# Two pairs of local attention and gated MLP on one core: Q and K of three blocks computed up front, and the head sums of block 0 made on VectorE

## The chip, the cores and the metric

The kernel runs on one core of one Trainium2 chip. The metric is the device time of one execution in microseconds. Before the change it is 1622.94 us, the median of 9 runs (1622.45 to 1624.91).

## The reference

There are two layers with residuals, A and B, and the pair runs twice over the same x of shape [1, 2048, 1024] in bf16:

```python
qkv = (x @ wqkv).reshape(B, S, 3, H, Dh)       # H = 32 heads of Dh = 32
idx = pos[:, None] - arange(8)[None, :] * 2    # W = 8 keys at distance 0, 2, ... 14
logits = einsum("bhsd,bhswd->bhsw", q, k[idx]) * Dh ** -0.5
attn = softmax(where(idx >= 0, logits, -1e9))
A(x) = einsum("bhsw,bhswd->bhsd", attn, v[idx]) @ wo
B(x) = ((x @ W_gate) * (x @ W_gate > 0) * (x @ W_up)) @ W_down     # F = 3584
x = x + A(layernorm(x));  x = x + B(layernorm(x))      # and both once more
```

A position sees only 8 keys behind it, so the scores are no matrix product: for each head, position and key 32 products are made and summed.

## The kernel before

**Tiling.** The 2048 tokens are cut into 4 blocks of 512 (NB = 4, four tiles of 128 tokens each). A block of one pair is a number n: 0 to 3 are the first pair, 4 to 7 the second (NN = 8). A PE group is eight matmuls of 128x128 by 128x512, which together give one 128x512 accumulator out of six in PSUM. x stays in SBUF. Weights come in slabs of 1 MB through a ring of five buffers (`wring`, `slab_events` L213).

**Attention of a block.** `ln_steps` (L225) normalizes the tiles, on ScalarE or for some on VectorE (`ln_dve_stats` L279, its reciprocal root on GpSimd at L294), and a DMA transposes the result to `xnT`. `qk_steps` (L464) makes 8 chunks of Q and 8 of K, one PE group each, with ScalarE copying q (L479) and k (L483) out of PSUM, and GpSimd copying the 14 columns of halo that a K chunk takes from the block before and leaves for the next (L485 to L488). `v_steps` makes V, which goes through DRAM (`v_d`) to a head-major layout (`load_v_steps` L617).

The scores are sums over 32 rows out of the eight chunks. Each row of a chunk holds one of 4 slices of a head, so the sum over chunks can be made elementwise, and the last sum over 4 rows on PE with the 0/1 matrix `sel`, or by two sums on VectorE after a trip through DRAM. There are three variants:

- block 0: `prod_direct_steps` (L509) makes one bf16 product of 128x4096 for each chunk on VectorE, and PE sums all eight with `sel` (`red_mm` L494, two times four chunks of eight matmuls);
- block 1: `prod_sum_steps` (L530) makes float32 products of half that size and adds them up on VectorE in two halves (L546, L548, L558). The last addition writes the bf16 tile `s`, and PE sums this with one `red_mm`;
- later blocks: the same sums, then `s` goes to DRAM and comes back in another layout (`store_s` L562, `load_s` L567, called s4 there), and VectorE adds the four slices (`head_sum` L578).

Then `softmax_steps` (L585), `pv_steps` (L631: products with V and their sums on VectorE), and the way through DRAM (`o_d`, `store_o` L659, `load_o` L668) to `oT`, which the output projection `wo_steps` (L679) needs.

**MLP of a block.** `gu_steps` (L702) runs 28 pairs of a gate group and an up group. ScalarE makes r = relu(gate), VectorE multiplies with up into `hT` (L103 on the page). `down_steps` (L727) sums over the 28 chunks of `hT` in two halves of D and adds the result to x (L758).

**The order of the work.** Each step is a Python function with a planned time. `emit` (L778) sorts all steps by it and calls them. Each engine therefore gets its instructions in this order, and some queues are held to it strictly: PE (`pe_group`, `mm`, L122 to L130), SyncE, which issues nearly all DMAs (`sp_dma` L113 to L119), and those VectorE instructions that go through `dv` (L98 to L103). The others are placed by a scheduler. The plan counts 1.73 us for a PE group (`GRP` L782). The order of the PE stages is: V0, QK0, QK1, V1, V2, output projection 0, V3, gate/up 0, QK2, output projection 1, down 0, gate/up 1, QK3, output projection 2, down 1, gate/up 2, QK4, V4, output projection 3, down 2, and so on. The schedule is at L788 to L913.

Of the kernel before, what the change touches and what calls it, by code (L numbers as in the profile page):

```python
# [13 lines left out]
P = 128  # L14
# [22 lines left out]
def kernel(  # L37
# [46 lines left out]
    pool = {}  # L84
    early_guard = tc.tile_pool(name="early", bufs=3)
    pool["early"] = early_guard.__enter__()

    def start_hidden():
        early_guard.__exit__(None, None, None)
        del pool["early"]  # L90
        pool["hid"] = ctx.enter_context(tc.tile_pool(name="hid", bufs=1))
# [19 lines left out]
    gate = [None]  # L111
# [45 lines left out]
    o_d = dram.tile([NT, H, DH, P], BF16, name="o_d")  # L157
    s_d = [dram.tile([P, W * BLK], BF16, name=f"s_d{i}") for i in range(2)]
# [31 lines left out]
    def want_qk(key, end):  # L190
        for i, nm in enumerate(("q", "k")):
            for hh in range(2):
                want((key, nm, hh), wqkv_v[:, hh * (KC // 2):(hh + 1) * (KC // 2), i * D:(i + 1) * D], end)
# [12 lines left out]
    def want_down(n, at, gap):  # L206
        for half in range(2):
            for s in range(NSL):
                rows = slice(8 * s, min(8 * (s + 1), FC))
                end = at + gap * (half * FC + min(8 * (s + 1), FC))  # L210
                want(("d", n, half, s), wd_v[:, rows, half * SLAB:(half + 1) * SLAB], end)
# [13 lines left out]
    def ln_steps(n, which, early=False, dve=()):  # L225
# [3 lines left out]
        def stats(t):  # L229
            def f():  # L230
# [6 lines left out]
                if t in dve:  # L237
                    hold[t] = ln_dve_stats(xt, which == "a")
                    return
# [11 lines left out]
        def apply(t):  # L251
            def f():
                if t in dve:
                    mv, rstd = hold[t]
                    if which == "a":
                        dv(nc.vector.tensor_scalar, hold["xn"][:, t, :], x_tiles[b * TPB + t][:], mv[:, 0:1], rstd[:],
                           op0=ALU.subtract, op1=ALU.mult)
                        return
                    gate[0] = nc.vector.tensor_scalar(hold["xn"][:, t, :], x_tiles[b * TPB + t][:], mv[:, 0:1], rstd[:],
                                                      op0=ALU.subtract, op1=ALU.mult).ins  # L260
                    return
# [17 lines left out]
    def ln_dve_stats(xt, ordered):  # L279
        def run(f, *args, **kwargs):  # L280
            if ordered:
                dv(f, *args, **kwargs)
            else:
                f(*args, **kwargs)

        bst = stat_pool.tile([P, 2, 6], F32, tag="bst", name="bst")
        run(nc.vector.bn_stats, bst[:, 0, :], xt[:, 0:512])
        run(nc.vector.bn_stats, bst[:, 1, :], xt[:, 512:1024])
        mv = stat_pool.tile([P, 2], F32, tag="mv", name="mv", bufs=4)
        run(nc.vector.bn_aggr, mv[:], bst[:].rearrange("p a b -> p (a b)"))  # L290
        vpe = stat_pool.tile([P, 1], F32, tag="vpe1", name="vpe1")
        run(nc.vector.tensor_scalar, vpe[:], mv[:, 1:2], EPS, None, op0=ALU.add)
# [171 lines left out]
    def qk_steps(n, ln, key):  # L464
        b = n % NB
        st = att[n]

        def f_(nm, c):
            def f():
                if nm == "q" and c == 0:  # L470
                    khalo[n] = qk_pool.tile([P, KC, HALO], BF16, tag="kh", name=f"kh_{n}", bufs=2)
# [5 lines left out]
                if nm == "q":  # L477
                    q = qk_pool.tile([P, BLK], BF16, tag="q", name=f"q_{n}_{c}")
                    tail_act[0] = nc.scalar.copy(q[:], acc[:]).ins  # L479
                    st[("q", c)] = q  # L480
                else:
                    k = qk_pool.tile([P, HALO + BLK], BF16, tag="k", name=f"k_{n}_{c}")
# [6 lines left out]
                    st[("k", c)] = k  # L489
            return f  # L490

        return [f_(nm, c) for nm, c in (QK_FIRST if n == 0 else QK_ORDER)]

    def red_mm(n, prod, first, last):  # L494
        st = att[n]
        if first:
            st["L"] = psum_l.tile([P, W, P], F32, tag="L", name=f"L_{n}")
        with pe_group():
            for wh in range(2):
                for tq in range(TPB):  # L500
                    mm(st["L"][32 * tq:32 * tq + 32, WH * wh:WH * (wh + 1), :], lhsT=sel[:],
                       rhs=prod[:, WH * wh:WH * (wh + 1), tq * P:(tq + 1) * P],
                       start=first, stop=last, skip_group_check=True, tile_position=(0, 32 * tq))
# [4 lines left out]

    def prod_direct_steps(n):  # L509
        prods = {}  # L510

        def mult(c):
            def f():
                if c in (3, 4):
                    prods[c] = work.tile([P, W, BLK], BF16, tag="t", name=f"prod_{c}")
                else:
                    prods[c] = big_tile([P, W, BLK], f"prod_{c}")
                i0, i1 = qk_bcast(n, c, 0, W)
                dv(nc.vector.tensor_tensor, prods[c][:], i0, i1, op=ALU.mult)
            return f  # L520

        def red(c0, c1):
            def f():
                for c in range(c0, c1):
                    red_mm(n, prods.pop(c), c == 0, c == KC - 1)
            return f

        return [mult(c) for c in range(KC)], [red(0, KC // 2), red(KC // 2, KC)]

    def prod_sum_steps(n):  # L530
        st = att[n]

        def mult(h, c):
            def f():
# [9 lines left out]
                if n == 1:  # L544
                    with tc.issue_after(gate[0]):
                        nc.vector.tensor_tensor(t[:], i0, i1, op=ALU.mult)  # L546
# [8 lines left out]
        def add(h, c):  # L555
            ac, t = st["ac"], st.pop(("t", c))
            o = st["s"][:, WH * h:WH * (h + 1), :] if c == KC - 1 else ac[:]
            nc.vector.tensor_tensor(o, ac[:], t[:], op=ALU.add)  # L558
# [72 lines left out]
    def pv_steps(n):  # L631
# [14 lines left out]
        def adds(g0):  # L646
            def f():
# [6 lines left out]
                gate[0] = tail_dve[0]  # L654
# [24 lines left out]
    def wo_steps(n):  # L679
# [3 lines left out]
        if n > 0:  # L683
            order = [(t, half) for half in range(2) for t in range(TPB)]

        def f_(i):
            def f():
                for t, half in order[2 * i:2 * i + 2]:
                    xt = x_tiles[b * TPB + t]
                    acc = psum.tile([P, BLK], F32, tag="acc", name="acc_wo")  # L690
                    with pe_group():
                        for c in range(KC):
                            mm(acc[:], lhsT=st["oT"][:, c, t, :], rhs=slab[("o", n, half)][:, c, :],
                               start=(c == 0), stop=(c == KC - 1))
                    xs = xt[:, half * SLAB:(half + 1) * SLAB]
                    nc.vector.tensor_tensor(xs, acc[:], xs, op=ALU.add)  # L696
            return f

        return [f_(t) for t in range(TPB)]


    def gu_steps(n, ln):  # L702
        hold = {}

        def f_(j):
            def f():
# [3 lines left out]
                accs = {}  # L710
                for nm in ("g", "u"):
# [5 lines left out]
                    accs[nm] = acc  # L717
                    if nm == "g":
                        r = pool["hid"].tile([P, BLK], BF16, tag="r", name="r", bufs=3)
                        with tc.issue_after(tail_exp[0]):  # L720
                            tail_act[0] = nc.scalar.activation(r[:], acc[:], ACT.Relu).ins  # L721
                dv(nc.vector.tensor_tensor, hold["hT"][:, j, :], accs["u"][:], r[:], op=ALU.mult)
            return f

        return [f_(j) for j in range(FC)], hold

    def down_steps(n, hold):  # L727
# [3 lines left out]
        def f_(half, s8):  # L731
            cols = [(t, 0, SLAB) for t in range(TPB)]
            if n == NN - 1 and half == 1:
                cols[-1:] = [(TPB - 1, 0, SLAB // 2), (TPB - 1, SLAB // 2, SLAB)]

            def f():
# [8 lines left out]
                ac = accs[half]  # L745
                nfc = min(8, FC - 8 * s8)
                wsl = slab[("d", n, half, s8)]
                for a, (t, c0, c1) in zip(ac, cols):
# [5 lines left out]
                if s8 == NSL - 1:  # L754
                    for a, (t, c0, c1) in zip(ac, cols):
                        xt = x_tiles[b * TPB + t]
                        xs = xt[:, half * SLAB + c0:half * SLAB + c1]
                        nc.vector.tensor_tensor(xs, a[:, c0:c1], xs, op=ALU.add)  # L758
                        if n == NN - 1:
                            row = (b * TPB + t) * P  # L760
                            col = half * SLAB + c0
                            dst = out_dram[row:row + P, col:col + c1 - c0]
                            if half == 1 and t % 2 == 1 and c0 == 0:
                                nc.scalar.dma_start(dst, xs)
                            else:
                                sp_dma(dst, xs)
            return f

        return [f_(half, s8) for half in range(2) for s8 in range(NSL)]
# [12 lines left out]
    GRP = 1.73  # L782

# [19 lines left out]
    def ln2(n, ats, turn_at=None, dve=()):  # L803
        stats, apply, turn, hold = ln_steps(n, "b", False, dve)
        ln_b[n] = hold
        for t, a in enumerate(ats):
            ev.append((a, stats[t]))
            ev.append((a + (4.0 if n == 0 else 12.0), apply[t]))
            if turn_at is None:
                ev.append((ats[-1] + 1.0 + 1.3 * t, turn(t)))  # L810
        if turn_at is not None:
            ev.append((turn_at, turn()))


    GAP0 = 1.9
    t_v0 = 9.5
    t_qk0 = t_v0 + GRP * KC
    t_qk1 = t_qk0 + GAP0 * 2 * KC
    t_v1 = t_qk1 + GRP * 2 * KC + 1.5
    t_v2 = t_v1 + GRP * KC  # L820
    t_wo0 = t_v2 + GRP * KC
    t_v3 = t_wo0 + GRP * KC
    t_gu0 = t_v3 + GRP * KC

    want_v("v0", t_v0 + GRP * 5, t_qk0)
    want_qk("qk01", t_v1)
    want_v("v123", t_v3 + GRP * KC / 2, t_gu0)
    for at, f in v_first(ln_a[0]):
        ev.append((t_v0 + at, f))
    ev.append((t_v0 + GRP * 5 + 0.5, lambda: load_x(1)))  # L830
# [3 lines left out]
    for t in range(TPB):  # L834
        ev.append((t_qk0 + (1.0, 2.0, 2.2 * GAP0, 4.2 * GAP0)[t], stats[t]))
        ev.append((t_qk0 + (1.9 + 2 * t) * GAP0 - 0.1, apply[t]))
        ev.append((t_qk0 + (1.9 + 2 * t) * GAP0, turn(t)))
    ev.append((t_qk0 + 1.5, store_v(0)))
    ev.append((t_qk0 + 18.0, lambda: load_x(3)))
    spread(qk_steps(0, ln_a[0], "qk01"), t_qk0, GAP0)  # L840
    mults, reds = prod_direct_steps(0)
    for c in range(KC):
        ev.append((t_qk0 + GAP0 * (2 * c + 2.0), mults[c]))
# [103 lines left out]
```

## Time and profile before

| | |
|---|---|
| median of 9 runs | 1622.94 us |
| the profiled execution | 1623.03 us |
| its span, first to last instruction | 1621.3 us |
| granted TensorE clock | 1.00 of full |
| DMA moved | 309.39 MB, 191 GB/s |
| `prod` of block 0 on VectorE | 8 x 2290 ns |
| `pv` products with V | 64 x 2286 ns |
| `x` plus output projection | 64 x 684 ns |
| gate product `hT` | 224 x 688 ns |

The profile is one execution with every instruction's start and length. A page gives each engine's busy time and share of the span, the chain of work that ended last (followed back from the last instruction, at each step to what released it), and groups of instructions by line, engine and tile. A group reads: line, engine, operation, output <- inputs, partitions x elements and type, count | busy us, mean ns | idle us of the engine just before them and what ended most of it. A timeline line reads: start us, length us, engine, line, operation, tiles, shape, count, and in brackets the idle time before it. Where a helper such as `mm` (L130) or `dv` (L103) records everything, all have its line, and the tile's name tells them apart. PE lengths overlap, since matmuls are pipelined: starts are to be compared with starts.

### The profile page before, as it was taken

To read this page: it belongs to the slowest core of one execution; us is meant where nothing else is said; L and a number is where in the kernel's file an instruction comes from. 1 tells how busy PE (TensorE), PEld (TensorE's weight loads), DVE (VectorE), ACT (ScalarE), POOL (GpSimd) and SP (SyncE) were. 2 spreads that over 40 slices of the span, in tenths; PEclk is the share of its full clock that TensorE was granted. 3 is DMA by queue.
4 is the path that set the end of the run, shared out by engine and by line. 5 is a ranking of instruction groups with operands and counts; after the bars stand their busy time and mean duration, and the time that the engine had idled before them with its cause. 6 is when DMAs were issued, how large, how long until landed. Compare 5 with 4: busy or idle time off the path is not lost.

```text
span 1621.3 us, 18791 instructions
## 1 busy us (share of the span) xinstructions
PE 1614.9 (100%) x7618; PEld 785.5 (48%) x7618; DVE 1085.4 (67%) x939; ACT 506.2 (31%) x1051; POOL 250.7 (15%) x220
## 2 busy tenths in 40 slices
PE   9999999999999999999999999999999999999999
PEld 6644445444544445444454444544445444444444
DVE  5799799959496857929579294892949929411211
ACT  4764323513252313613136031360313301131110
POOL 2321006400351002200053000530005100000000
PEclk9999999999999999999999999999999999999999
DMA  9589556776479585684757947579574894655452
GB/s 301 111 210 241 163 175 201 192 208 207 130 216 227 156 234 180 181 225 157 224 179 188 241 152 225 159 204 248 171 227 155 199 252 157 208 165 173 156 166 68
DMA packets 398006, 309.39 MB, mean 191 GB/s; under 512 B 167648, under 2 KB 377952, under 8 KB 396256
## 3 DMA queue, kind: packets, MB, share of 16 engines
q1 hardware_dynamic: 397344, 307.62, 66.9%
q8 instruction: 59, 0.97, 0.3%
q10 hardware_dynamic: 576, 0.59, 0.1%
q14 instruction: 27, 0.22, 0.0%
HBM read 263.06 MB, written 27.29 MB: 179 GB/s over the span
## 4 chain that ended last, share of the span: by engine, by line
PE 99%; DMA 0%; SPq 0%; issue 0%; DVE 0%; DVEq 0%
PE acc_g L130 24%; PE acc_u L130 24%; PE dacc L130 18%; PE acc_v L130 7%; PE acc_q L130 7%; PE acc_k L130 7%; PE acc_wo L130 7%; PE dacc_pair L130 6%; DMA w_v<-in_A_wqkv_dram 0%; PE L L130 0%; PE tp L366 0%; SPq L119 0%; DVE x L758 0%; SPq L116 0%; DVEq L942 0%
## 5 line engine op out<-in xcount | busy, mean ns | idle before, releaser
L130 PE MATMUL acc_g<-xnT_b,w_g 128*128 128x512 bf16 x1792 | 423.3, 379 | 0.0
L130 PE MATMUL acc_u<-xnT_b,w_u 128*128 128x512 bf16 x1792 | 423.3, 379 | 0.0
L721 ACT ACTIVATE r<-acc_g 128x512 bf16<-128x512 f32 x224 | 133.2, 597 | 713.3 <-PE acc_g L130 707.6
L103 DVE TENSOR_TENSOR hT<-acc_u,r 128x512 bf16<-128x512 f32 x224 | 151.8, 688 | 285.7 <-PE acc_u L130 272.2
L130 PE MATMUL dacc<-w_d,hT 128*128 128x512 bf16 (+1 forms) x1400 | 301.6, 375 | 0.0
L130 PEld LDWEIGHTS <-hT 128*128 128x128 bf16 x1820 | 178.1, 98 | 209.0
L130 PEld LDWEIGHTS <-w_g 128*128 128x128 bf16 x1792 | 175.3, 98 | 211.6 <-issue 0.4
L130 PEld LDWEIGHTS <-w_u 128*128 128x128 bf16 x1792 | 175.3, 98 | 211.4
L488 POOL COPY kh<-k 128x14 bf16<-128x14 bf16 x64 | 89.3, 1400 | 742.4 <-ACT k L483 742.3
L548 DVE TENSOR_TENSOR t<-q,k 128x2048 f32<-128x2048 bf16 x84 | 192.0, 2293 | 8.7 <-ACT k L483 5.7
L558 DVE TENSOR_TENSOR ac<-ac,t 128x2048 f32<-128x2048 f32 x84 | 191.9, 2284 | 0.4
L103 DVE TENSOR_TENSOR pv<-a,vhm 128x4096 bf16<-128x4096 bf16 x64 | 143.6, 2286 | 0.0
L758 DVE TENSOR_TENSOR x<-dacc,x 128x512 bf16<-128x512 f32 (+1 forms) x50 | 32.2, 676 | 159.0 <-PE dacc L130 159.0
L103 DVE TENSOR_TENSOR pv<-pv 128x1024 bf16<-128x1024 bf16 (+1 forms) x128 | 113.8, 952 | 0.0
L130 PE MATMUL acc_wo<-w_o,oT 128*128 128x512 bf16 x512 | 111.8, 379 | 0.0
L130 PE MATMUL dacc_pair<-w_d,hT 128*128 128x512 bf16 x420 | 95.9, 379 | 0.0
L247 POOL TENSOR_TENSOR st_b<-st_b,neg_half 128x1 f32<-128x1 f32 x29 | 48.1, 1670 | 282.6 <-ACT st_b L246 282.6
L130 PEld LDWEIGHTS <-oT 128*128 128x128 bf16 x512 | 50.1, 98 | 60.3
L487 POOL COPY k<-kh 128x14 bf16<-128x14 bf16 x48 | 68.3, 1424 | 68.4 <-DVE t L548 43.8
L479 ACT CAST q<-acc_q 128x512 bf16<-128x512 f32 x64 | 37.4, 585 | 74.3 <-PE acc_q L130 74.3
L242 ACT ACTIVATE xn_b<-x 128x1024 bf16<-128x1024 bf16 x29 | 30.3, 1047 | 90.2 <-DVE x L696 90.2
L483 ACT CAST k<-acc_k 128x512 bf16<-128x512 f32 x64 | 37.4, 584 | 60.5 <-PE acc_k L130 60.5
(137 smaller groups left out, 1231.6 us busy)
## 6 DMA issues: line engine op xcount, KB each, us to landing
w_g<-in_B_W_gate_dram SPq DMA_DIRECT2D x56, 1024.0 KB, 6.9
w_u<-in_B_W_up_dram SPq DMA_DIRECT2D x56, 1024.0 KB, 5.5
w_d<-in_B_W_down_dram SPq DMA_DIRECT2D x48, 1024.0 KB, 5.7
w_o<-in_A_wo_dram SPq DMA_DIRECT2D x16, 1024.0 KB, 7.0
vhm<-v_d SPq DMA_DIRECT2D x32, 284.0 KB, 6.8
v_d<-vT SPq DMA_DIRECT2D x8, 1024.0 KB, 10.1
oT<-o_d SPq DMA_DIRECT2D x32, 256.0 KB, 4.3
w_d<-in_B_W_down_dram SPq DMA_DIRECT2D x16, 512.0 KB, 3.9
```

The lines of the kernel that those rows point to most:

```text
L103: tail_dve[0] = f(*args, **kwargs).ins
L130: tail_pe[0] = nc.tensor.matmul(*args, **kwargs).ins
L242: nc.scalar.activation(xn, xt[:], ACT.Square, accum_out=sq)
L247: nc.gpsimd.tensor_tensor(rstd, vpe, neg_half[:, 0:1], op=ALU.pow)
L479: tail_act[0] = nc.scalar.copy(q[:], acc[:]).ins
L483: tail_act[0] = nc.scalar.copy(k[:, HALO:HALO + BLK], acc[:]).ins
L487: nc.gpsimd.tensor_copy(k[:, 0:HALO], khalo[n - 1][:, c, :])
L488: nc.gpsimd.tensor_copy(khalo[n][:, c, :], k[:, BLK:BLK + HALO])
L548: nc.vector.tensor_tensor(t[:], i0, i1, op=ALU.mult)
L558: nc.vector.tensor_tensor(o, ac[:], t[:], op=ALU.add)
L721: tail_act[0] = nc.scalar.activation(r[:], acc[:], ACT.Relu).ins
L758: nc.vector.tensor_tensor(xs, a[:, c0:c1], xs, op=ALU.add)
```

## The change

Three things are done.

1. Block 0's scores are made as those of block 1: `prod_sum_steps(0)` on VectorE in float32, and one selector set (`head_mm`, 8 matmuls instead of 2 x 32).
2. Q and K of blocks 1, 2 and 3 are computed in the early stages. Each chunk is copied to one of six staging buffers, put into DRAM (`q_d`, `k_d`) and got back shortly before its sums (`put` and `get`: 48 of each). One set of Q/K weight slabs serves blocks 2 and 3 (`qk23`), where there were two.
3. The order of the early PE stages becomes: V0, QK0, QK1, V1, V2 with the selector set of block 0 after its third group, V3, 22 of the 32 groups of QK2 and QK3, output projection 0, the other 10 groups, gate/up 0 with the selector set of block 1 after its 11th pair, down 0 first half, output projection 1, down 0 second half, gate/up 1, down 1 first half, output projection 2, down 1 second half, gate/up 2. From there on the PE order is as before. The softmax of blocks 2 and 3 is planned 28.6 us later within gate/up 1 and 2, behind sums of the same block that reach into this stage.

For the blocks of the first pair the sums, the x additions and the normalization on VectorE now go through `dv`, in the order of the plan. x of block 1 is loaded at the plan's time 0.35, right behind the first four slabs, and its normalization on VectorE moves from QK0 into V0. The diff's core:

```diff
+    stage_guard = tc.tile_pool(name="stage", bufs=6)
+    pool["stage"] = stage_guard.__enter__()
...
+    q_d = [dram.tile([KC, P, BLK], BF16, name=f"q_d{n}") for n in range(1, NB)]
+    k_d = [dram.tile([KC, P, HALO + BLK], BF16, name=f"k_d{n}") for n in range(1, NB)]
...
-    def qk_steps(n, ln, key):
+    def qk_steps(n, ln, key, staged=False):
...
+        def tile_of(nm, c, cols):
+            if staged:
+                t = pool["stage"].tile([P, HALO + BLK], BF16, tag="st", name=f"{nm}st_{n}_{c}")
+                staging[nm, c] = t[:, 0:cols]
+                return t[:, 0:cols]
+            t = qk_pool.tile([P, cols], BF16, tag=nm, name=f"{nm}_{n}_{c}")
+            st[(nm, c)] = t
+            return t[:]
...
+        def put(nm, c):
+            def f():
+                sp_dma((q_d if nm == "q" else k_d)[n - 1][c], staging.pop((nm, c)))
+            return f
+
+        def get(nm, c):
+            def f():
+                t = qk_pool.tile([P, BLK if nm == "q" else HALO + BLK], BF16, tag=nm, name=f"{nm}_{n}_{c}")
+                st[(nm, c)] = t
+                sp_dma(t[:], (q_d if nm == "q" else k_d)[n - 1][c])
+            return f
...
-    def red_mm(n, prod, first, last):
+    def head_mm(n):
         st = att[n]
-        if first:
-            st["L"] = psum_l.tile([P, W, P], F32, tag="L", name=f"L_{n}")
+        st["L"] = psum_l.tile([P, W, P], F32, tag="L", name=f"L_{n}")
         with pe_group():
             for wh in range(2):
                 for tq in range(TPB):
                     mm(st["L"][32 * tq:32 * tq + 32, WH * wh:WH * (wh + 1), :], lhsT=sel[:],
-                       rhs=prod[:, WH * wh:WH * (wh + 1), tq * P:(tq + 1) * P],
-                       start=first, stop=last, skip_group_check=True, tile_position=(0, 32 * tq))
+                       rhs=st["s"][:, WH * wh:WH * (wh + 1), tq * P:(tq + 1) * P],
+                       start=True, stop=True, skip_group_check=True, tile_position=(0, 32 * tq))
...
-                if n == 1:
-                    with tc.issue_after(gate[0]):
-                        nc.vector.tensor_tensor(t[:], i0, i1, op=ALU.mult)
+                if n < NB:
+                    dv(nc.vector.tensor_tensor, t[:], i0, i1, op=ALU.mult)
...
-            nc.vector.tensor_tensor(o, ac[:], t[:], op=ALU.add)
+            if n < NB:
+                dv(nc.vector.tensor_tensor, o, ac[:], t[:], op=ALU.add)
+            else:
+                nc.vector.tensor_tensor(o, ac[:], t[:], op=ALU.add)
...
+    ahead = 2 * KC + 6
+    t_wo0 = t_qk2 + GRP * ahead
+    t_fill = t_wo0 + GRP * KC
+    t_gu0 = t_fill + GRP * (4 * KC - ahead)
...
+    want_qk("qk23", t_qk2 + GRP * 2 * KC, t_gu0)
...
-    ev.append((t_v0 + GRP * 5 + 0.5, lambda: load_x(1)))
+    ev.append((0.35, lambda: load_x(1)))
...
-        ev.append((t_qk0 + (1.0, 2.0, 2.2 * GAP0, 4.2 * GAP0)[t], stats[t]))
+        ev.append((t_v0 + 7.5 + 2.0 * t, stats[t]))
...
-    mults, reds = prod_direct_steps(0)
-    for c in range(KC):
-        ev.append((t_qk0 + GAP0 * (2 * c + 2.0), mults[c]))
-    ev.append((t_qk0 + GAP0 * 10.5, reds[0]))
+    spread(prod_sum_steps(0), t_qk0 + 3.5, 4.4)
...
+    ev.append((t_v2 + 2.2 * GRP, lambda: head_mm(0)))
+    spread(softmax_steps(0), t_v2 + 2.3 * GRP, 0.01)
+    t_pv0 = t_v2 + 2.2 * GRP + 10.0
+    spread(pv_steps(0), t_pv0, 4.3)
...
+    steps = qk2[0::2] + qk3[0::2] + qk2[1::2] + qk3[1::2]
+    puts = puts2[0::2] + puts3[0::2] + puts2[1::2] + puts3[1::2]
+    spread(steps[:ahead], t_qk2, GRP)
+    spread(puts[:ahead], t_qk2 + GRP + 1.2, GRP)
+    spread(steps[ahead:], t_fill, GRP)
+    spread(puts[ahead:], t_fill + GRP + 1.2, GRP)
+    place(wo_steps(0), t_wo0)
...
+    spread(sums1[:4], t_pv0 + 34.5, 4.5)
+    spread(sums1[4:6], t_wo0 + 1.0, 6.0)
+    spread(sums1[6:10], t_fill + 1.4, 4.6)
+    spread(sums1[10:], t_gu0 + 2.6, 5.4)
+    spread(load_v_steps(1), t_wo0 + 4.0, 7.0)
+    t_head1 = t_gu0 + 37.0
+    ev.append((t_head1, lambda: head_mm(1)))
...
+            spread(gets2, at + 36.0, 2.5)
+            spread(prod_sum_steps(2), t_head1 + 11.5 + 44.5, 5.0)
         elif n + 1 < NN:
-            ev.append((at - 3.1, store_s(n + 1)))
-            ev.append((at + 0.4, load_s(n + 1)))
-            spread(softmax_steps(n + 1), at + 14.0, 3.6)
-            spread(pv_steps(n + 1), at + 25.0, 6.0)
+            t_s = at + (29.0 if n < NB - 1 else 0.4)
+            ev.append((t_s - (6.0 if n < NB - 1 else 3.5), store_s(n + 1)))
+            ev.append((t_s, load_s(n + 1)))
+            spread(softmax_steps(n + 1), t_s + 13.6, 3.6)
+            spread(pv_steps(n + 1), t_s + 24.6, 6.0)
...
+            if n == 1:
+                spread(gets3, at + 24.0, 2.5)
+                spread(prod_sum_steps(3), t_s + 76.0, 4.9)
...
+        middle = n + 2 < NB
+        if middle:
+            want_down(n, 0, at, GRP / 2)
+            place(downs[0], at)
+            at += GRP * FC / 2
```

## The prediction

> **What bounds the kernel now.** I read the busy times and the chain of waits of the page first: they say which engine sets the end.
>
> ```profile
> PE 1614.9 (100%) x7618; PEld 785.5 (48%) x7618; DVE 1085.4 (67%) x939; ACT 506.2 (31%) x1051; POOL 250.7 (15%) x220
> ...
> PE 99%; DMA 0%; SPq 0%; issue 0%; DVE 0%; DVEq 0%
> ```
>
> TensorE works without a gap from 10.05 us to about 1618, so a gain can only come from matmuls taken away, and a loss only from a new hole in PE. The second view is the PE timeline around the selector products: one set of 32 in block 0 (there are two, at 43.98 and 58.06), then block 1's single set of 8.
>
> ```profile
> 42.16 1.89 PE L130 MATMUL acc_q<-xnT_first,w_qk_q 128*128 128x512 bf16 x8
> 43.98 1.91 PE L130 MATMUL L<-prod,sel 128*32 128x512 bf16 x32
> 45.82 1.95 PE L130 MATMUL acc_k<-xnT_first,w_qk_k 128*128 128x512 bf16 x8
> 47.60 1.89 PE L130 MATMUL acc_q<-xnT_first,w_qk_q 128*128 128x512 bf16 x8
> ...
> 192.91 1.89 PE L130 MATMUL acc_u<-xnT_b,w_u 128*128 128x512 bf16 x8
> 194.73 0.61 PE L130 MATMUL L<-s,sel 128*32 128x512 bf16 x8
> 195.28 1.90 PE L130 MATMUL acc_g<-xnT_b,w_g 128*128 128x512 bf16 x8
> ```
>
> An ordinary group of eight costs 1.73 us from start to start. The large set adds 47.60 - 42.16 - 2 x 1.73 = 1.98 us; the small one 195.28 - 192.91 - 1.73 = 0.64 us.
>
> The third view is VectorE by form and in its timeline. It is not the bound over the span, but it is nearly full early: 54.3 of the 57 us from 55 to 112 and 90.4 of the 100 us from 140 to 240 are busy. The change puts its new work there.
>
> ```profile
> L548 DVE TENSOR_TENSOR t<-q,k 128x2048 f32<-128x2048 bf16 x84 | 192.0, 2293 | 8.7 <-ACT k L483 5.7
> L558 DVE TENSOR_TENSOR ac<-ac,t 128x2048 f32<-128x2048 f32 x84 | 191.9, 2284 | 0.4
> ...
> L103 DVE TENSOR_TENSOR prod<-q,k 128x4096 bf16<-128x4096 bf16 x8 | 18.2, 2290 | 6.5 <-ACT k L483 3.7 <-POOL k L485 2.8
> ```
>
> ```profile
> 134.72 2.29 DVE L558 TENSOR_TENSOR ac<-ac,t 128x2048 f32<-128x2048 f32 x1
> 137.11 2.29 DVE L546 TENSOR_TENSOR t<-q,k 128x2048 f32<-128x2048 bf16 x1
> 139.32 2.29 DVE L558 TENSOR_TENSOR ac<-ac,t 128x2048 f32<-128x2048 f32 x1
> ```
>
> A float32 operation does half the elements of the bf16 product in the same 2.29 us, and a product with its sum advances the queue by 139.32 - 134.72 = 4.60 us.
>
> **PE: removed and added.** Two sets of 32 go, one set of 8 comes: -2 x 1.98 + 0.64 = -3.3 us. All other groups (Q, K, V, output, gate, up, down) keep their number and shape; the new order only permutes them. So -3.3 us, 0.2% of the span, is the whole gain there can be. One set of Q and K weights is fetched for blocks 2 and 3 instead of two: 4 MB less. That is worth nothing, because no slab sets a PE wait now.
>
> **Block 0 on VectorE, the first wait.** Eight products (18.2 us) become 16 products and 14 sums, about 68 us. The first K chunk is ready at about 29.2 (before, the first product starts at 29.66, behind LayerNorm work of block 1 that now lies in v0). The next two follow K at two groups, 3.45 us, each. From the fourth, at 40.7, VectorE is late. The last sum of the first half then starts at 40.7 + 5 x 4.60 - 0.2 = 63.5. The second half needs 15 instructions, 33.9 us by the 2.20 between starts plus the extra 0.19 on five of them, so its last sum starts at 97.5 and ends at 99.8, up to 1.4 later by halo copies and the semaphore. PE starts Q/K of block 0 at 24.89, runs 32 groups (55.3), eight of v1 (13.8) and three of v2 (5.2), and comes to the selector set at 99.2. It stands in PE's fixed queue, so everything behind waits: 0.4 to 2.0 us, I take 1.2.
>
> What follows has cover. Softmax took 8.2 us and the value products 34.2 in before (60.02 to 102.41), so they end near 143.5. The stores of `o_d` keep that pace, and the `oT` loads are in by about 154; the output projection, behind v3 and 22 Q/K groups, comes at 111.8 + 51.8 - 3.3 + 1.2 = 161.5. If that cover of 7 us were gone, its excess would be a PE hole.
>
> **Block 1 on VectorE, the second wait.** Call G the start of gate/up 0; it follows the output projection (13.8) and ten Q/K groups (17.3), that is 31.1 us. VectorE can do eight instructions of block 1's sums before the projection and is then held by the x additions and LayerNorm in a queue now written out by hand. Call W the projection's start, so G is W + 31.1. From the second half of tile 1's x, at W + 7.1, I add the queue up: x additions 0.6 each, LayerNorm 2.84 a tile (1.63 without the last xn), t plus sum 4.4 to 4.6. The last xn is done at W + 26.7, and its transpose, which took 3.1 us from issue in before (134.39 to 137.53), lands 0.6 us ahead of G: no wait, 0 to 1. The rest of the sums, with seven to eight gate products of 0.6 between them, ends at W + 71.1 to 72, that is G + 40.0 to 40.9. PE comes to the set after eleven gate/up pairs, at G + 38.0 (before, at 194.73, the scores had been ready since about 188.6). This is a wait of 1.5 to 4 us; I take 2.7. Queued behind it on PE is all of gate/up, and on VectorE softmax 1, which has the output projection of block 1 a half of down 0 later to cover it.
>
> **Puts, gets and halo copies.** 48 stores and 48 loads of 128 KB, less the 4 MB saved, stand in SP's one queue among the slab issues. The stores wait for ACT's copy or POOL's halo. Six staging buffers cover six groups, 10.4 us, while the 256 KB store of `o_d` took 2.3 us: no wait of PE. The one place where it is close is the fill: 13 halo copies stand on POOL behind the reciprocal root of tile 3, and the put of a late K chunk stands in SP ahead of slab w_u_1, which PE needs at G + 15.5.
>
> ```profile
> 253.19 2.26 POOL L488 COPY kh<-k 128x14 bf16<-128x14 bf16 x1
> 255.39 2.26 POOL L487 COPY k<-kh 128x14 bf16<-128x14 bf16 x1
> 257.59 0.19 POOL L488 COPY kh<-k 128x14 bf16<-128x14 bf16 x1
> ```
>
> A halo copy costs 0.19 or 2.26 us, the latter as long as a VectorE operation beside it; 13 of them took 16.3 us (253.05 to 269.38), 1.26 each. At that pace the slab is issued at G + 4 and lands at about G + 9.5: nothing. At 2.26 each it is issued at G + 13.3 and lands near G + 18.6: 3.1 us of hole. That would mostly replace the second wait, since it lets VectorE catch up.
>
> The Trainium skill, "SBUF — State Buffer", section "Who interferes with whom", speaks against the change: a VectorE operation with two SBUF inputs and a GpSimd operation that reads SBUF exclude each other for a whole instruction. Taken as one copy per VectorE operation, its sum would be the slower of the two above, 3.1; the rows show that short copies slip between.
>
> **Gate/up 2, the third place.** Block 3's sums now end in gate/up 2, and its scores take the way through `s_d` (8.5 us median to landing) 28.6 us later. I put the last part's landing at 48.3 us into the stage, 5.7 past its planned time, with softmax ahead of gate products in VectorE's queue and PE's six accumulators as the cover. The slack is 0.4; the wait 0 to 1, taken as 0.4. Block 2's scores in gate/up 1 are moved alike, but its sums are planned 12 us earlier against their stage: nothing. The x tiles of block 1, now loaded ahead of K's slabs, put the last K slab at 27.1 against a need at 27.6: 0 to 0.5, taken as nothing.
>
> **Sum.** 1623.03 (the profiled execution, 0.1 above the median) - 3.3 + 1.2 + 2.7 + 0.4 = 1624.0.
>
> **Rivals.** No wait at either set: if VectorE's queue is 1 to 3 us quicker than my sum, only -3.3 is left, 1619.7. For it: pairs with less semaphore time, since the sums are now in one chain. Against it: two places where my sum ends after PE's arrival, both by rows of this trace.
>
> Slower, by block 3's scores: every microsecond by which `s` of block 3 lands beyond 48.7 into gate/up 2 holds the gate products, then the accumulators, then PE. VectorE carries 50 us more before it, and block 2 and 3's sums were moved from beside Q/K to beside gate/up and down, where gate products cut in at 0.69 each. If sums or the `s_d` trip (issued behind gets and slabs) are 4 us late, the price is 3.6 and the time 1627.6; at 8 us, 1631. It decides from 2.6 us late (1624.0 + 2.2 = 1626.2). For it: SP's queue is shared and its waits are long; against it: before, VectorE sat idle for 159 us ahead of the x additions of the down stages, where it can catch up.
>
> That the edit doesn't do what it says can be left aside: the PE program has 112 instructions fewer, 56 matmuls and their weight loads.
>
> **How the numbers follow.** The two waits, forecast: 0.46, own range 1622 to 1626.2. No wait: 0.17. Late scores: 0.37, its price being the least known. About 0.2%, 3.2 us, is what a measurement of this kernel tells from no change: faster needs under 1619.7, which is where the rival without a wait lies, so 0.11 of its chance goes there and 0.06 to no change, giving 0.52 for that. For 8 in 10 I go from 1619.5 (nothing can be much below) to 1631.
>
> **What would show it.** PE has a hole before the selector set near 99 of about 1 us and one near G + 38 of 2 to 4, and DVE `s` is their releaser. The sets are x8 with 0.64 each. No hole before the output projection of block 0. In gate/up 2 a hole, if any, follows DVE hT behind softmax. I am wrong if the sums' pair is not 4.6, if a slab is the releaser of a PE hole, or if a hole stands at a transpose.

## The result: 1630.96 us, 0.49% slower

The changed kernel takes 1630.96 us (median of 9 runs, 1630.30 to 1631.93), against 1622.86 of the kernel before (29 runs): a ratio of 1.0049, 95% interval 1.0041 to 1.0058. Its profiled execution took 1631.03 us, 8.0 more than that of before. The page of after, its busy times and the first line of its chain:

```profile
PE 1613.8 (99%) x7562; PEld 784.4 (48%) x7562; DVE 1135.5 (70%) x961; ACT 476.7 (29%) x971; POOL 228.8 (14%) x212
...
PE 97%; DMA 1%; POOL 0%; issue 0%; ACT 0%; SPq 0%; DVE 0%; DVEq 0%; ACTq 0%; POOLq 0%
```

The 56 matmuls are gone, and VectorE works 50 us more, as forecast. But PE's share of the chain falls from 99% to 97%, and DMA has 1% of it. Two places do it. A hole is counted here from the start of one matmul to the start of the next, less the 0.216 us that a step ordinarily takes. The chain of waits of after, around the first (start us, us, what):

```profile
78.24 0.11 POOL kst L488
...
80.22 2.21 POOL kst L488
...
82.44 0.32 SPq L121
...
82.85 0.38 SPq L121
...
83.36 5.61 DMA w_v<-in_A_wqkv_dram
88.97 0.05 issue
89.02 2.98 PE acc_v L132 x13
```

PE waits 1.96 us, between matmuls that start at 86.85 and 89.02, for the second V slab. SP issued it at 83.36, behind puts of K chunks of block 1, which waited for halo copies (L488) on GpSimd. The second place, in the same view and in ScalarE's timeline:

```profile
200.35 1.74 PE acc_g L132 x8
...
202.22 0.52 SPq L121
...
202.84 7.81 DMA k_d<-kst
...
210.80 0.61 ACT r L722
211.41 0.04 issue
211.45 3.44 PE acc_g L132 x8
```

```profile
193.88 0.59 ACT L484 CAST kst<-acc_k 128x512 bf16<-128x512 f32 x1 [0.65 <-DMA k_d<-kst]
210.80 1.57 ACT L722 ACTIVATE r<-acc_g 128x512 bf16<-128x512 f32 x3 [16.33 <-DMA k_d<-kst]
```

Three pairs of gate/up 0 run, then PE stops for 7.81 us, because the first relu, whose accumulator was ready near 195, starts only at 210.80. What released it is the landing of the last put of K into DRAM. That put was issued at 202.84, right behind two slabs of 1 MB (201.11 and 202.22), and took 7.8 us to land. The puts of block 1 took 1.7 to 2.5 us with no slab ahead of them (72.22 to 74.40, for one), and the last of them, issued at 86.99 behind four slabs, 11.67.

The stretches of after around this hole (length, busy us of PE, PEld, DVE, ACT, POOL, then the granted clock and DMA):

```profile
203.00:211.40 8.40, 0.81 (x4) 0.29 (x3) 1.67 (x1) 0.60 (x2) 1.86 (x2) 0.79 0.83 264
211.40:214.80 3.40, 3.35 (x9) 1.20 (x9) 3.37 (x3) 0.98 (x3) 0.00 (x0) 0.52 0.00 0
214.80:225.00 10.20, 10.20 (x49) 4.64 (x48) 10.20 (x8) 1.79 (x3) 0.00 (x0) 1.00 0.65 206
```

After the hole PE runs at 0.52 of its clock: eight matmuls stand up to 0.43 us apart instead of 0.216, 1.55 us lost. The account closes: -3.3 + 1.96 + 7.81 + 1.55 = +8.0. At the two selector sets, where the forecast had its waits, there is no hole: PE came to them late enough by now.

The sums of block 0 run as forecast, in VectorE's timeline of after with 4.63 us for a product and its sum (45.42 to 50.05), and beside them, in GpSimd's, the halo copies take as long as a sum:

```profile
45.42 2.29 DVE L106 TENSOR_TENSOR t<-q,k 128x2048 f32<-128x2048 bf16 x1
47.63 2.29 DVE L106 TENSOR_TENSOR ac<-ac,t 128x2048 f32<-128x2048 f32 x1
50.05 2.29 DVE L106 TENSOR_TENSOR t<-q,k 128x2048 f32<-128x2048 bf16 x1
```

```profile
71.08 2.26 POOL L489 COPY kh<-kst 128x14 bf16<-128x14 bf16 x1
73.29 2.26 POOL L488 COPY kst<-kh 128x14 bf16<-128x14 bf16 x1
75.50 0.19 POOL L489 COPY kh<-kst 128x14 bf16<-128x14 bf16 x1
```

### The profile page after: what moved, and what is told of

Same layout as the page of the kernel before. It is cut to its first block, busy times and chain, and to the rows that moved or that the text cites. A ratio compares the mean times of both kernels' runs of the same rounds, so it can differ in the third digit from the quotient of the medians.

```text
span 1629.3 us, 18825 instructions
## 1 busy us (share of the span) xinstructions
PE 1613.8 (99%) x7562; PEld 784.4 (48%) x7562; DVE 1135.5 (70%) x961; ACT 476.7 (29%) x971; POOL 228.8 (14%) x212
## 4 chain that ended last, share of the span: by engine, by line
PE 97%; DMA 1%; POOL 0%; issue 0%; ACT 0%; SPq 0%; DVE 0%; DVEq 0%; ACTq 0%; POOLq 0%
PE acc_g L132 24%; PE acc_u L132 24%; PE dacc L132 18%; PE acc_wo L132 7%; PE acc_q L132 6%; PE acc_k L132 6%; PE acc_v L132 6%; PE dacc_pair L132 6%; DMA w_v<-in_A_wqkv_dram 1%; DMA k_d<-kst 1%; POOL st_a L249 0%; SPq L121 0%; POOL kst L488 0%; ACT xn_a L245 0%; PE L L132 0%
## 5 line engine op out<-in xcount | busy, mean ns | idle before, releaser
L541 DVE TENSOR_TENSOR t<-q,k 128x2048 f32<-128x2048 bf16 x56 | 128.0, 2292 | 6.7 <-ACT k L484 4.6
L769 DVE TENSOR_TENSOR x<-dacc,x 128x512 bf16<-128x512 f32 (+1 forms) x38 | 24.5, 673 | 154.1 <-PE dacc L132 154.1
L106 DVE TENSOR_TENSOR t<-q,k 128x2048 f32<-128x2048 bf16 x56 | 127.6, 2288 | 4.0 <-ACT k L484 2.4
L489 POOL COPY kh<-k 128x14 bf16<-128x14 bf16 x40 | 53.7, 1348 | 510.2 <-ACT k L484 510.2
L249 POOL TENSOR_TENSOR st_b<-st_b,neg_half 128x1 f32<-128x1 f32 x29 | 39.4, 1366 | 522.3 <-ACT st_b L248 522.3
L554 DVE TENSOR_TENSOR ac<-ac,t 128x2048 f32<-128x2048 f32 x48 | 109.7, 2285 | 0.3
L106 DVE TENSOR_TENSOR ac<-ac,t 128x2048 f32<-128x2048 f32 x48 | 109.6, 2284 | 0.0
L410 ACT CAST vT<-acc_v 128x512 bf16<-128x512 f32 x56 | 32.7, 585 | 58.6 <-PE acc_v L132 58.6
```

The source lines that it names most:

```text
L106: tail_dve[0] = f(*args, **kwargs).ins
L249: nc.gpsimd.tensor_tensor(rstd, vpe, neg_half[:, 0:1], op=ALU.pow)
L410: tail_act[0] = nc.scalar.copy(st["vT"][:, c, :], acc[:]).ins
L489: nc.gpsimd.tensor_copy(khalo[n][:, c, :], k[:, BLK:BLK + HALO])
L769: run = dv if n < NB - 2 else (lambda f, *args, **kwargs: f(*args, **kwargs))
```

## Experiments

### The staging memory: is it what holds the relu?

`late_pool` stages the last two K chunks of block 3 in two buffers that stay where they are:

```diff
+    late = ctx.enter_context(tc.tile_pool(name="late", bufs=2))
...
-                t = pool["stage"].tile([P, HALO + BLK], ...)
+                where = late if (n, nm) == (3, "k") and c >= KC - 2 else pool["stage"]
+                t = where.tile([P, HALO + BLK], ...)
```

> The last two K chunks of block 3 are staged in two buffers of a pool of their own, so that the gate/up tiles no longer lie where the last puts are read from. Theory M (the first relu waits for memory: its tile is taken from the pool that follows the staging pool, and this is held by the last put, which landed at 210.66): the hole of 7.81 us at 203.4 goes, and with it the 1.6 us of half-clock matmuls behind it; in its place PE waits for block 1's s at its selector set, by my sum 2.7 us. Time 1631.0 - 7.8 - 1.6 + 2.7 = 1624.3 (1623 to 1625.5). Rival S (the late gate/up slabs issued behind the puts set the hole, and the relu's wait is only what the trace puts it down to): the puts and slabs are issued as before, so the hole stays and the time is 1631.

Measured: 1624.73 us, ratio 1.0013 (1.0003 to 1.0022). The hole of 7.81 is 1.76 and there is no half clock, although the two slabs are issued later than in the change (203.34 and 203.84) and the last put lands later still, at 213.04; the wait at block 1's set came back with 1.31 (3.07 together, expected 2.7). The relu no longer waits for a put:

```profile
204.33 1.09 ACT L724 ACTIVATE r<-acc_g 128x512 bf16<-128x512 f32 x2 [10.20 <-POOL kh L491]
```

It now waits for the last halo copy that reads the old staging buffers, so GpSimd's lateness is the rest of it.

`relu_pool` gives the relu's tiles a pool that never held staging buffers, and moves block 1's set two pairs later:

```diff
+    rpool = ctx.enter_context(tc.tile_pool(name="relu", bufs=3))
...
-                        rs[j] = pool["hid"].tile([P, BLK], BF16, tag="r", name="r", bufs=3)
+                        rs[j] = rpool.tile([P, BLK], BF16, tag="r", name="r")
...
-    t_head1 = t_gu0 + 37.0
+    t_head1 = t_gu0 + 44.0
```

> The relu's three tiles r come from a pool of their own that never held staging buffers; hT stays where it is, over them, and block 1's selector set stands two pairs later. If the first relu waits because its pool was opened in the place of the staging pool (and not for bytes of its own or for a late accumulator), r starts at once, near 195, and only the first gate product on VectorE waits for the last put's landing at 210.7. PE then runs on until its six accumulators are held, four and a half pairs into gate/up 0, near 208.7, and stops for 2.7 us instead of 7.8, with no half clock: 1631.0 - 7.8 - 1.6 + 2.7 = 1624.3. If the relu waits for something else, hole and time stay: 1631.

Measured: 1626.67 us, ratio 1.0027 (1.0018 to 1.0037). ScalarE's and PE's timeline:

```profile
195.01 0.60 ACT L723 ACTIVATE r<-acc_g 128x512 bf16<-128x512 f32 x1 [0.82 <-PE acc_g L133]
```

```profile
211.76 3.17 PE L133 MATMUL acc_u<-xnT_b,w_u 128*128 128x512 bf16 x8 [2.97 <-DVE hT L107]
```

The relu starts at 195.01 although the last put lands at 210.54 as ever. PE runs one and a half pairs further and stops for the gate product, which writes hT over the staging buffers. The wait belongs to the pool that takes the place of another, not to the relu. The time is 2.4 above the 1624.3: the hole is 3.13, not 2.7, and half clock followed it after all (1.3 us).

### The put: late by itself, or by what is ahead of it?

`put_first` moves one event, so that the last put goes ahead of the two slabs:

```diff
-    spread(puts[ahead:], t_fill + GRP + 1.2, GRP)
+    spread(puts[ahead:-1], t_fill + GRP + 1.2, GRP)
+    ev.append((t_gu0 + 0.1, puts[-1]))
```

> The last put of K stands ahead of the two gate/up slabs in SP's queue instead of behind them; nothing else is moved. If its landing 7.8 us after issue is due to the 2 MB ahead of it, it lands about 2 us after issue, near 205, the first relu starts some 6 us earlier, the hole is about 2 us, there is no half clock behind it, and the wait for s of block 1 comes back with 1 to 2.5 us: 1625 to 1626. If the put is slow by itself, or if the slabs set the hole (they are issued 1 us later here), the time is 1631 to 1632.

Measured: 1624.89 us, ratio 1.0012 (1.0002 to 1.0021). The put, the third in the first line below, is issued at 202.50 and lands at 204.75; the hole is 1.98 and the wait at block 1's set 1.31. SP's queue and ScalarE's timeline:

```profile
195.89 6.92 SPq L121 DMA_DIRECT2D k_d<-kst  x3
202.92 0.39 SPq L121 DMA_DIRECT2D w_u<-in_B_W_up_dram  x1
203.40 0.58 SPq L121 DMA_DIRECT2D w_g<-in_B_W_gate_dram  x1
```

```profile
204.90 0.60 ACT L722 ACTIVATE r<-acc_g 128x512 bf16<-128x512 f32 x1 [10.22 <-POOL kh L489]
```

One DMA moved past two others is worth 6 us. The last halo copy on GpSimd ends only at 204.8 too, so this is as much as the order of the queue can give here.

### GpSimd's halo copies

`halo_act_n1` and `halo_act_all` make the halo copies of staged chunks on ScalarE, the first for block 1 only:

```diff
-                        nc.gpsimd.tensor_copy(k[:, 0:HALO], khalo[n - 1][:, c, :])
-                    nc.gpsimd.tensor_copy(khalo[n][:, c, :], k[:, BLK:BLK + HALO])
+                        halo(k[:, 0:HALO], khalo[n - 1][:, c, :])
+                    halo(khalo[n][:, c, :], k[:, BLK:BLK + HALO])
```

with `halo = nc.scalar.copy if staged else nc.gpsimd.tensor_copy` (`staged and n == 1` in the first).

> The halo copies of block 1's K chunks run on ScalarE instead of GpSimd. Theory P (GpSimd's copies wait for VectorE's sums, the puts wait for them, and the V slab waits behind the puts in SP's queue): the hole of 1.95 us at 86.9 goes, and PE comes to block 0's selector set ahead of s, which was done at 100.5: a wait of about 1.2 us there. The second hole is untouched. 1631.0 - 1.95 + 1.2 = 1630.2. Rival (the slab is late because SP is held by transposes and by the puts' own waits for ScalarE, which this change makes longer): the hole stays or grows, 1631 to 1632.

Measured: 1629.96 us, ratio 1.0044 (1.0029 to 1.0059). The V slab is issued at 79.48 instead of 83.36, the hole at 86.9 is gone, and the wait for s at block 0's set stands uncovered, 1.02 us in all:

```profile
99.04 0.40 PE L132 MATMUL L<-s,sel 128*32 128x512 bf16 x4
100.28 0.40 PE L132 MATMUL L<-s,sel 128*32 128x512 bf16 x4 [0.84 <-DVE s L106]
```

> All halo copies of the staged K chunks (blocks 1 to 3) run on ScalarE, none on GpSimd. Theory P: the puts follow ScalarE's copies at once, so neither the V slab nor the first relu is late. Both holes go, with the half clock, and what is left are the two waits for s of the forecast, now uncovered: 1.2 us at block 0's set and 2.7 us at block 1's. 1623.0 - 3.3 + 1.2 + 2.7 = 1623.6 (1622.8 to 1624.5). Rival: ScalarE's extra copies delay the evictions and the puts as much as GpSimd did, and holes of 2 us or more stay at the V slab or the first relu: 1625 or more.

Measured: 1627.17 us, ratio 1.0026 (1.0016 to 1.0036). This one missed by 3.6. The copies end at 193.8, but the hole in the fill is still 5.31 us with 1.85 of half clock behind it. The timeline of SP's queue shows why:

```profile
192.14 1.84 SPq L121 DMA_DIRECT2D k_d<-kst  x4
194.07 0.43 SPq L121 DMA_DIRECT2D w_u<-in_B_W_up_dram  x1
194.60 0.60 SPq L121 DMA_DIRECT2D w_g<-in_B_W_gate_dram  x1
195.29 4.06 SPq L121 DMA_DIRECT2D k_d<-kst  x1
```

The last put is issued 7.5 us earlier than in the change, so ScalarE's copies do not delay it as the rival had it. But it still stands behind the slabs and lands at 207.39, 12.1 us after issue. In the second hole GpSimd is only part of the cause; the order in SP's queue is the larger.

`halo_act_heads` adds block 0's set (and its softmax) one group later and block 1's two pairs later, on top of `halo_act_all`:

```diff
-    ev.append((t_v2 + 2.2 * GRP, lambda: head_mm(0)))
+    ev.append((t_v2 + 3.2 * GRP, lambda: head_mm(0)))
...
-    t_head1 = t_gu0 + 37.0
+    t_head1 = t_gu0 + 44.0
```

> As before it, and block 0's selector set stands one PE group later (after four of V2), block 1's two gate/up pairs later (after 13). If VectorE's lateness at the two sets was all that was left, PE has no hole above 0.3 us after the start and only the saved matmuls count: 1623.0 - 3.3 = 1619.7, 0.2% faster than the kernel before. If softmax and what follows from the later sets becomes late in its turn (output projection, gate products), 1621 to 1624.

Measured: 1625.99 us, ratio 1.0022 (1.0012 to 1.0032). No wait at either set, but the hole in the fill stays for the same reason, 4.83 us and 2.8 of half clock.

### The clock

`warm_hole` puts dummy work into the hole (30 extra matmuls, whose result is not used):

```diff
+                if n == 0 and j == 3:
+                    scratch(30)
                 for nm in ("g", "u"):
...
-    t_head1 = t_gu0 + 37.0
+    t_head1 = t_gu0 + 44.0
```

> 30 matmuls on constants are put into PE's queue ahead of the group that waited in the second hole (6.5 of its 7.8 us), and block 1's selector set is moved two pairs later so that PE can use what it gains. If the 0.43 us matmuls behind the hole come from the idle time, the eight of them take 0.22 each, and the time falls by about 1.6 us, to 1629.4. If they come from something else (the wait's end, the DMA traffic), they stay at 0.43 and the time at 1631.

Measured: 1629.36 us, ratio 1.0041 (1.0026 to 1.0056). PE's idle time is 1.23 us here, the group behind it runs at full clock, and the time falls by the 1.6 us:

```profile
211.14 1.89 PE L132 MATMUL acc_g<-xnT_b,w_g 128*128 128x512 bf16 x8 [1.06 <-ACT r L724]
```

The half clock is a price of idle time, not of what ended it.

### One part of the change alone

`direct0` keeps the early Q and K, and makes block 0's scores as before (`prod_direct_steps` and `red_mm` back in, `head_mm(0)` out):

```diff
-    spread(prod_sum_steps(0), t_qk0 + 3.5, 4.4)
+    mults, reds = prod_direct_steps(0)
+    for c in range(KC):
+        ev.append((t_qk0 + GRP * (2 * c + 2.0), mults[c]))
+    ev.append((t_qk0 + GRP * 11.0, reds[0]))
+    ev.append((t_qk1 + 2.0 * GRP, reds[1]))
```

> Q and K up front as in the change, but block 0's scores made as before: eight bf16 products on VectorE and two selector sets of 32. If the first hole comes from VectorE's float32 sums standing in the way of GpSimd's halo copies, the copies of block 1's chunks take 0.2 us and the hole at 86.9 goes, while PE has the 3.3 us of selector matmuls again; the second hole, in the fill, lies beside block 1's sums and stays with its half clock. 1631.0 - 1.95 + 3.3 = 1632.4. If the halo copies are slow whatever VectorE does, the first hole stays: 1634.3.

Measured: 1632.73 us, ratio 1.0063 (1.0049 to 1.0077). Without sums beside them the copies are short in GpSimd's timeline:

```profile
63.98 0.19 POOL L489 COPY kh<-kst 128x14 bf16<-128x14 bf16 x1 [4.66 <-ACT kst L484]
64.11 0.20 POOL L488 COPY kst<-kh 128x14 bf16<-128x14 bf16 x1
```

The hole at 86.9 is gone, but this run does not show why: the two large sets make PE itself some 4 us later there, and the slab lands at 88.44, hardly earlier than in the change. The clean test of that hole is `halo_act_n1`.

### All causes together

`halo_put` is `halo_act_all` with the edit of `put_first`; `halo_put_heads` has the later sets as well.

> Halo copies of the staged chunks on ScalarE and, with them, the last put of K ahead of the two gate/up slabs in SP's queue. With the copies on ScalarE alone the last put was issued at 195.3 and landed at 207.4, behind 2 MB of slabs. If this queueing is the rest of the second hole, the put lands near 201, ahead of PE's need at 202.9, the hole and the half clock are gone, and the two waits for s that the forecast summed stand alone: 1 us at block 0's set and 2.7 us at block 1's, 1623.6 (1622.8 to 1624.4). If another user of the staging memory holds the relu, a hole of several us stays: 1625 to 1627.

Measured: 1624.66 us (1622.61 to 1626.82), ratio 1.0012 (1.0003 to 1.0021). The hole in the fill is gone: the last put lands at 200.54, the first relu starts at 200.69, in time for PE. (The put still took 6.2 us from its issue at 194.34, with no slab ahead of it; why is not shown.) PE waits 0.4 us at 27.2 for the last K slab, the place that the forecast had as 0 to 0.5 and took as nothing. Otherwise the two waits of the forecast are what is left, 1.01 us at block 0's set and 2.22 at block 1's:

```profile
230.84 0.40 PE L132 MATMUL L<-s,sel 128*32 128x512 bf16 x4
233.28 0.40 PE L132 MATMUL L<-s,sel 128*32 128x512 bf16 x4 [2.05 <-DVE s L106]
233.62 2.69 PE L132 MATMUL acc_g<-xnT_b,w_g 128*128 128x512 bf16 x8
236.10 2.83 PE L132 MATMUL acc_u<-xnT_b,w_u 128*128 128x512 bf16 x8
```

The last two lines should read 1.89: here too, behind a hole of 2.2 us, half clock costs 1.8. That is why the median lies a microsecond above the 1623.6, and why the runs spread: those whose mean clock was 1.000 took 1622.6 and 1622.9, the others 1624.3 to 1626.8.

> The same with block 0's selector set one PE group later and block 1's two gate/up pairs later. If VectorE's lateness is all that is left, no hole remains and the saved selector matmuls show: 1623.0 - 3.3 = 1619.7, a ratio of 0.998 to the kernel before. If the waits only move (softmax, output projection, scores of blocks 2 and 3), 1621 to 1623.6.

Measured: 1619.93 us (1619.23 to 1620.31), ratio 0.9981 (0.9973 to 0.9990). PE has no step over 0.31 us from the first Q matmul to the last one except where records are missing. Between these two it takes 1615.01 - 25.22 = 1589.79 us, against 1618.02 - 24.89 = 1593.13 before: -3.34. From 190 to 245, around the fill and block 1's set, the chain of waits is PE alone:

```profile
by line: PE acc_g L132 48.9%; PE acc_u L132 47.1%; PE acc_k L132 3.5%; PE L L132 1.0%
```

This version beats both kernels, the one before by 0.19%, with the change's idea intact.

## Why the prediction was right and wrong

The sum of 1624.0 missed by 7 us, and so did the outcome held likeliest, no clear change. One of the prediction's own signs of being wrong came true: a slab, `w_v`, is the releaser of a PE hole (89.02). The two holes that it told of, near 99 and near G + 38, are not in the changed kernel.

**PE's gain.** Right: -3.3 forecast, -3.34 shown by `halo_put_heads`.

**The waits for s.** Right in mechanism and near in size, but covered in the changed kernel. Forecast 1.2 and 2.7; uncovered, `halo_put` shows 1.01 and 2.22. Its s of block 1 comes 40.5 us after the start of gate/up 0 (192.76 to 233.28), within the 40.0 to 40.9 of the working. In the changed kernel the hole ahead of each set took its place, so these two terms are not in its +8.0.

**The step that failed** is "Puts, gets and halo copies", in its "no wait of PE" and in the fill's "nothing". Three things in it:

- The halo copies were priced only in the fill. In Q/K of block 1, where the sums of block 0 now keep VectorE full, many of them stretched from 0.2 to 2.3 us, held the puts, and these the V slab: 1.96 us, shown by `halo_act_n1`.
- In the fill I asked when slab w_u_1 lands, and that was answered rightly: issued 7.8 us into gate/up 0, between the 4 and 13.3 of the working, and landed at 14.1, ahead of its need at 15.5. But I did not ask who waits for the put that is behind it. The diff closes the staging pool and opens `hid` in its place (`start_hidden`), so the first relu and the first gate product wait for every reader of the staging buffers, the last put among them. I priced the last put by its issue; the only landing of a store that this step names is that of an `o_d` store, 2.3 us, where this put took 7.81. `late_pool`, `relu_pool` and `put_first` show the parts of it: the pool, and 6 us of queueing behind two slabs.
- The half clock after a long hole, 1.55 us, was in no term.

**The slower rival**, late scores of block 3 in gate/up 2, did not happen in the changed kernel: the last part of `s` lands 47.3 us into the stage (521.00 to 568.33; the working had 48.3), and PE has no step above 0.31 us behind block 1's set. So the 0.4 of the sum is 0. But two of the variants show its mechanism:

```profile
572.99 2.29 DVE L106 TENSOR_TENSOR u<-s 128x2048 f32<-128x2048 bf16 x1 [7.59 <-DMA s<-s_d]
580.88 1.89 PE L132 MATMUL acc_u<-xnT_b,w_u 128*128 128x512 bf16 x8 [0.74 <-DVE hT L106]
```

These are VectorE's and PE's lines of `direct0`, where `s` lands 49.8 us into the stage and PE waits 0.91 us for a gate product. In `warm_hole` it lands at 49.4 and PE waits 0.48; in all other runs of the change at 47.3 to 47.5, with no wait. The working let the wait begin at 48.7, a microsecond for a microsecond, which gives 1.1 and 0.7. What made `s` late in these two is not shown.

**The rival without a wait** is where `halo_put_heads` ends, at 1619.9 for 1619.7, but it needed four edits that the change did not have.

The measured time lies inside the range, at its very edge, and on the slower side that the late scores had been given. That is luck: the range held it through the price of another mechanism, not through an understanding of this one.

## What to carry to other kernels

When a pool is opened where another was closed, its first writers can wait for the readers of the old one, as the relu and the gate product did here; list them. Price a store by its landing and by what is ahead of it in the DMA queue: the store of 131.5 KB behind 2 MB of weights landed with the weights here (210.66 us, the second slab at 210.28). Where results that something waits for share a queue with prefetches, try the results first. And a wait that is removed uncovers the next: four edits were needed here before the 3.3 us showed.

## What the hardware showed that was not expected

Idle time and the clock of PE, one execution each (times in us; the half clock is read from the granted clock in the traces):

| hole | run | PE again at | half clock from, to | steps over 0.30 behind it | lost |
|---|---|---|---|---|---|
| 7.81 | the changed kernel | 211.45 | 207.80, 214.63 | 8 | 1.55 |
| 7.76 | halo_act_n1 | 210.26 | 206.98, 213.81 | 9 | 1.74 |
| 7.64 | direct0 | 212.15 | 207.72, 217.96 | 14 | 2.85 |
| 5.31 | halo_act_all | 208.19 | 205.15, 211.97 | 9 | 1.85 |
| 4.83 | halo_act_heads | 206.41 | 205.29, 212.12 | 14 | 2.80 |
| 3.13 | relu_pool | 211.76 | 210.98, 214.39 | 6 | 1.28 |
| 2.22 | halo_put | 233.28 | 234.57, 237.99 | 10 | 1.80 |
| 2.14 | relu_pool, at the V slab | 88.82 | none | 0 | 0.00 |
| 1.98 | put_first | 205.55 | none | 0 | 0.00 |

The loss does not follow the length of the hole. The half clock comes in stretches of 3.41, 6.83 or 10.24 us, one, two or three times 3.41. What is lost is half of that part of the stretch in which PE is at work again: in the changed kernel 214.63 - 211.45 = 3.18, half of it 1.59, and in every row within 0.1 us. In `halo_put` the stretch begins only 1.3 us after the hole has ended (granted clock, the third number from the end):

```profile
233.00:234.00 1.00, 0.71 (x6) 0.31 (x6) 1.00 (x3) 0.00 (x0) 0.00 (x0) 1.00 0.00 0
234.00:235.00 1.00, 1.00 (x6) 0.45 (x4) 1.00 (x3) 0.00 (x0) 0.00 (x0) 0.79 0.02 8
235.00:236.00 1.00, 1.00 (x4) 0.30 (x2) 1.00 (x2) 0.00 (x0) 0.00 (x0) 0.50 0.00 0
```

So the loss depends on where the hole lies against these stretches. A hole of 2.14 us cost nothing, one of 2.22 cost 1.80, and two of the eleven runs of `halo_put` kept a mean clock of 1.000. From which share of idle time the clock falls was not measured.

The Trainium skill, "TensorE: Matmul & The Clock Gate", section "What's actually happening", has the array fall to half rate after at least one idle window of about 3.4 us, the window running freely. The fall to half and the stretches in multiples of 3.41 us agree with the table; a hole of 2.2 us is shorter than that window and was enough in most runs of `halo_put`.
